# Chunk attention and HyperMixer on one Trainium2 core: 12 loads a batch, heads h and h+4 on two partition halves, block-diagonal v, three score units a batch, joint w_q/w_k projection

## The chip, the cores and the metric

One core of one Trainium2 chip. The metric is device time in microseconds of one execution. A profiled execution also gives the span from the first to the last instruction, which is about 2 us shorter. TensorE's clock is granted by a throttle; the profile shows it by slice of time.

## The reference, cut to what matters

```python
# q, k, v: (8 batches, 8 heads, 576, 64) float32
def _attn_ref(q, k, v):                       # chunks of 64, nine a head
    scores = scale * np.matmul(q_c, k_c.transpose(0, 1, 2, 4, 3))
    ...                                       # softmax over each chunk
    return np.matmul(attn, v_c)

def _moe_ref(x, w_q, w_k, w_out):             # x: (8, 576, 512)
    wq, wk = x @ w_q, x @ w_k                 # 512 -> 64 each
    W_tok = scale * np.einsum('bsd,btd->bst', wq, wk)
    mixed = np.einsum('bst,btd->bsd', W_tok, x)
    return np.maximum(mixed, 0.0) @ w_out     # 512 -> 512
```

The kernel does not form W_tok: it computes G = wk^T x first (64 x 512), then wq G. It works in float16 with float32 accumulation.

## The kernel before

The order of all work is fixed in a string, `PLAN`. A token is a unit, and the digit behind the colon is the slot of a ring of four PSUM tiles (128 x 2 x 512 float32) that it uses: `Tq00` transposes one part of q, `S` computes scores and the exponential, `A` multiplies by v and divides by the sum, `X` transposes, `Q`, `K`, `G` and `M` are the mixer up to the relu, `O` is one 128-row output block.

All inputs are loaded by GpSimd, which casts them to float16. A batch has 16 loads, each on all 128 partitions:

```python
def load_qk(b, part):                      # parts of 5 and 4 row blocks
    a, e = TR[part]
    for src, dst in ((qf, qn), (kf, kn)):
        for t in range(a, e, 2):           # rows of 1 KB
            x = min(t + 2, e)
            nc.gpsimd.dma_start(dst[b][part][:, t - a : x - a, :], ...[:, t:x, :])

def load_v(b, lo, hi):
    for t in range(lo, hi, 6):             # rows of 256 B
        nc.gpsimd.dma_start(vt[b][:, t : t + 6, 0:D], ...[:, t : t + 6, :])
```

An attend unit takes two heads. A chunk is a 64-row, 65-column matmul (64 columns of v and one of ones); rows and columns of the array are both used in halves, and a unit is 20 matmuls, two of them padding:

```python
for c in (2 * jj, 2 * jj + 1):
    half = CH * (g % 2)
    lhsT = est[...][half : half + CH, ...]
    rhs = vt[b][half : half + CH, g // 2, 0 : D + 1]
    nc.tensor.matmul(a[CH * (c % 2) : CH * (c % 2) + CH, hh, jj * W : jj * W + D + 1], lhsT=lhsT, rhs=rhs, ...)
```

Q is projected with a doubled w_q, so that both partition halves hold it; K takes another 20 matmuls a batch. The stores are issued by SyncE. They are held back until the last load has landed: a two-element transfer (`mark`) reads the last k tile first, on the same queue, so that stores never compete with loads. An output block is written over input tiles that are no longer needed.

```python
nc.scalar.copy(os_, a[:, 0, :])
if n == GATE:
    nc.sync.dma_start(mark[:], kn[B - 1][1][0:1, 0, 0:2])
nc.sync.dma_start(of[n * P : n * P + P, :], os_)
```

The softmax here doesn't subtract the row's maximum and nothing guards it: scores larger than these inputs give would overflow.

## Time and profile before

| | before |
|---|---|
| median of 3 runs | 136.05 us (134.57 to 137.67) |
| profiled span | 133.2 us |
| GpSimd issues loads until | 100.8 us |
| first output store | 104.4 us |
| TensorE ends | 127.6 us |

The page of the profile of before. First the busy time of each engine, then three of its rows over 40 slices of the span (busy tenths of TensorE, granted clock in tenths, GB/s moved), then the chain that ended last, by engine:

```profile
PE 107.0 (80%) x2479; PEld 65.6 (49%) x2479; DVE 77.7 (58%) x132; ACT 67.6 (51%) x117; POOL 97.8 (73%) x138
...
PE   6924397069999698999969987999999599999930
...
PEclk9995558965899975799999998699999999999995
...
GB/s 11 144 128 166 126 117 186 165 137 164 164 142 152 167 157 138 152 169 149 142 162 168 135 161 154 153 148 153 160 131 154 119 374 339 383 340 383 388 381 150
...
POOL 51%; PE 30%; DMA 9%; issue 3%; DVE 3%; ACT 0%; DVEq 0%; POOLq 0%
```

TensorE is busy 80% of the time, but the chain is 51% GpSimd (POOL). In the row of GB/s there are two regimes behind the start: about 120 to 190 GB/s (counted in float16, half of what is read) for four fifths of the span, then 340 to 390 GB/s of stores.

The timeline of GpSimd in before, one batch (start, duration, engine, line, operation, output and input, count; an idle time before the group would stand in brackets):

```profile
57.23 5.01 POOL L113 DMA_DIRECT2D vt<-in_v_dram  x6
62.11 1.54 POOL L106 DMA_DIRECT2D qn<-in_q_dram  x2
63.52 1.57 POOL L106 DMA_DIRECT2D kn<-in_k_dram  x2
64.94 2.16 POOL L106 DMA_DIRECT2D qn<-in_q_dram  x3
66.93 2.15 POOL L106 DMA_DIRECT2D kn<-in_k_dram  x3
68.89 5.11 POOL L113 DMA_DIRECT2D vt<-in_v_dram  x6
```

There is no idle time: the next load is issued as soon as the last one has been. From one v group to the next it is 11.66 us. The starts also give the time of one load: with 256 rows about 0.70 us, with 768 rows 0.81 us, so rows are cheap and instructions are dear.

The waits of before, on the engines and on the store queue (total us, times, longest):

```profile
DVE kT L153 <- DMA kn<-in_k_dram: 13.9, 13, 4.1
...
DVE qT L153 <- DMA qn<-in_q_dram: 11.5, 5, 4.3
```

```profile
SPq L314 <- DMA kn<-in_k_dram: 102.9, 1, 102.9
SPq L315 <- ACT rmx L288: 2.9, 5, 1.3
```

VectorE, which transposes q and k, waits 25.4 us for loads. The stores wait 102.9 us for the last k load. The first output store in the queue's timeline:

```profile
104.42 0.65 SPq L315 DMA_DIRECT2D out_dram<-qn  x1
```

### The profile page before, as it was taken

The page shows a single profiled execution, that of the slowest core. Times are in us where ns is not written, and L with a number is a line of the kernel's source. Part 1 is how long each engine was busy: PE and PEld are TensorE (multiplying, and loading weights), DVE is VectorE, ACT ScalarE, POOL GpSimd, SP SyncE. Part 2 cuts the span into 40 slices and gives each one's busy share as a digit, 9 for nine tenths or more (in the row PEclk, how much of TensorE's full clock was granted, in tenths as well). Part 3 has the DMA queues.
Part 4 walks back from the last instruction along what each step waited for, and adds up shares of the span by engine and source line. Part 5 has one row for each costly group of instructions (what it writes and reads, how often), then busy time and mean ns, then how long its engine had stood idle before and what let it go on. Part 6 is the DMA issues. An engine that isn't in the chain of part 4 may idle for free.

```text
span 133.2 us, 5640 instructions
## 1 busy us (share of the span) xinstructions
PE 107.0 (80%) x2479; PEld 65.6 (49%) x2479; DVE 77.7 (58%) x132; ACT 67.6 (51%) x117; POOL 97.8 (73%) x138
## 2 busy tenths in 40 slices
PE   6924397069999698999969987999999599999930
PEld 2303275054367346566746655557657276643400
DVE  3151685244888767697677967587895776500000
ACT  3003121037653655348637673558758367579830
POOL 6999996999999999999999999998992000000000
PEclk9995558965899975799999998699999999999995
DMA  0999999999999999999999999999999399999993
GB/s 11 144 128 166 126 117 186 165 137 164 164 142 152 167 157 138 152 169 149 142 162 168 135 161 154 153 148 153 160 131 154 119 374 339 383 340 383 388 381 150
DMA packets 64669, 24.69 MB, mean 185 GB/s; under 512 B 41092, under 2 KB 60036, under 8 KB 64644
## 3 DMA queue, kind: packets, MB, share of 16 engines
q0 software_dynamic: 59456, 14.89, 118.5%
q1 hardware_dynamic: 5188, 9.44, 19.0%
q8 instruction: 19, 0.31, 1.0%
q14 instruction: 6, 0.05, 0.1%
HBM read 29.75 MB, written 9.44 MB: 294 GB/s over the span
## 4 chain that ended last, share of the span: by engine, by line
POOL 51%; PE 30%; DMA 9%; issue 3%; DVE 3%; ACT 0%; DVEq 0%; POOLq 0%
POOL vt L113 22%; POOL qn L106 14%; PE ring L300 13%; POOL kn L106 13%; DMA wout<-in_moe_w_out_dram 5%; DMA kn<-in_k_dram 4%; PE ring L176 3%; PE ring L240 3%; PE ring L266 2%; PE ring L230 2%; PE ring L280 2%; PE ring L207 2%; DVE xt L235 2%; PE ring L252 1%; DVE kT L153 1%
## 5 line engine op out<-in xcount | busy, mean ns | idle before, releaser
L113 POOL DMA_DIRECT2D vt<-in_v_dram x48 | 40.5, 952 | 1.8 <-DMA wout<-in_moe_w_out_dram 1.2
L300 PE MATMUL ring<-wout,rmx 128*128 128x512 f16 x144 | 37.6, 400 | 0.2
L184 ACT ACTIVATE est<-ring 128x640 f16<-128x640 f32 (+1 forms) x32 | 19.3, 650 | 25.5 <-PE ring L176 24.7
L106 POOL DMA_DIRECT2D qn<-in_q_dram x40 | 29.9, 845 | 0.8 <-POOLq L348 0.8
L106 POOL DMA_DIRECT2D kn<-in_k_dram x40 | 30.0, 844 | 0.0
L153 DVE STREAM_TRANSPOSE kT<-kn 128x640 f32<-128x640 f32 (+1 forms) x16 | 19.4, 1215 | 14.0 <-DMA kn<-in_k_dram 13.9
L217 DVE TENSOR_TENSOR xn<-ring,rec 128x640 f16<-128x640 f32 x32 | 26.4, 824 | 1.2
L176 PE MATMUL ring<-qT,kT 32*64 32x64 f16 x1152 | 15.6, 215 | 13.4 <-DVE qT L153 4.9
L288 ACT ACTIVATE rmx<-ring 128x576 f16<-128x576 f32 x32 | 19.9, 653 | 5.0 <-PE ring L280 4.7
L176 PEld LDWEIGHTS <-kT 32*64 32x64 f16 x1152 | 13.6, 115 | 17.6 <-DVE kT L153 10.2
L300 PEld LDWEIGHTS <-rmx 128*128 128x128 f16 x144 | 12.9, 100 | 15.0 <-issue 3.4
L153 DVE STREAM_TRANSPOSE qT<-qn 128x640 f32<-128x640 f32 (+1 forms) x16 | 12.3, 770 | 11.8 <-DMA qn<-in_q_dram 11.5
L235 DVE COPY xt<-ring 128x1280 f16<-128x1280 f16 x16 | 12.8, 810 | 1.6 <-PE ring L230 1.5
L312 ACT COPY qn<-ring 128x512 f32<-128x512 f32 x16 | 9.4, 588 | 7.3 <-PE ring L300 5.9
L207 PE MATMUL ring<-vt,est 64*64 64x65 f16 x576 | 12.0, 211 | 1.3 <-ACT est L184 1.1
L230 PE MATMUL ring<-ident,xn 128*128 128x128 f16 x160 | 12.3, 230 | 0.4 <-DVE xn L217 0.3
L312 ACT COPY kn<-ring 128x512 f32<-128x512 f32 x16 | 9.4, 589 | 6.4 <-PE ring L300 6.2
L207 PEld LDWEIGHTS <-est 64*64 64x64 f16 x576 | 8.5, 120 | 7.3 <-issue 3.6
L247 ACT CAST wqT<-ring 128x576 f16<-128x576 f32 x8 | 5.1, 639 | 13.7 <-PE ring L240 13.7
L230 PEld LDWEIGHTS <-xn 128*128 128x128 f16 x160 | 10.3, 103 | 2.4 <-issue 0.6
L216 DVE RECIPROCAL rec<-ring 128x10 f32<-128x10 f32 x32 | 6.5, 202 | 7.6 <-PE ring L207 7.1
L240 PE MATMUL ring<-xt,wqd 128*128 128x288 f16 x64 | 9.7, 293 | 1.3 <-DVE xt L235 1.3
(30 smaller groups left out, 76.0 us busy)
## 6 DMA issues: line engine op xcount, KB each, us to landing
vt<-in_v_dram POOLq DMA_DIRECT2D x48, 96.0 KB, 4.2
qn<-in_q_dram POOLq DMA_DIRECT2D x32, 128.0 KB, 4.5
kn<-in_k_dram POOLq DMA_DIRECT2D x32, 128.0 KB, 4.6
out_dram<-qn SPq DMA_DIRECT2D x16, 256.0 KB, 3.7
out_dram<-kn SPq DMA_DIRECT2D x16, 256.0 KB, 3.7
out_dram<-spare SPq DMA_DIRECT2D x4, 256.0 KB, 3.4
qn<-in_q_dram POOLq DMA_DIRECT2D x8, 64.0 KB, 4.5
kn<-in_k_dram POOLq DMA_DIRECT2D x8, 64.0 KB, 4.3
```

The lines of the kernel that those rows point to most:

```text
L106: nc.gpsimd.dma_start(dst[b][part][:, t - a : x - a, :], src[b].rearrange("(t p r) d -> p t (r d)", p=P, r=R)[:, t:x, :],)
L113: nc.gpsimd.dma_start(vt[b][:, t : t + 6, 0:D], vf[b].rearrange("(t p) d -> p t d", p=P)[:, t : t + 6, :],)
L153: nc.vector.transpose(out=o, in_=src[b][part].bitcast(F32).rearrange("p t (r d) -> p t r d", d=32))
L176: nc.tensor.matmul(a[CH * ch : CH * ch + CH, i, (t - t0) * CH : (t - t0) * CH + CH], lhsT=k_of(b, t, 2 * rows + i, ch, e), rhs=q_of(b, t, ...
L184: nc.scalar.activation(est[b % 2][s].rearrange("p i t c -> p i (t c)")[:, :, 0:n], a[:, :, 0:n], AF.Exp, scale=scale_attn,)
L207: nc.tensor.matmul(a[CH * (c % 2) : CH * (c % 2) + CH, hh, jj * W : jj * W + D + 1], lhsT=lhsT, rhs=rhs, start=True, stop=True,)
L217: nc.vector.tensor_tensor(out=xn[b % 2][:, :, 2 * kk * D : 2 * kk * D + 2 * D].rearrange("p j (i d) -> p i j d", i=2), in0=xv[:, :, :, 0:D ...
L230: nc.tensor.transpose(tx[:, i, j * P : j * P + P], xn[b % 2][:, j, (2 * n + i) * P : (2 * n + i) * P + P], ident[:],)
L235: nc.vector.tensor_copy(xt[b % 2][n][:], tx[:, :, 0 : NJ * P])
L288: nc.scalar.activation(rmx[(b // 2) % 2].rearrange("p (h i) n -> p i h n", h=2)[:, i, :, o : o + HS], a[:, :, 0:HS], AF.Relu, scale=scale_moe,
L300: nc.tensor.matmul(a[:, 0, :], lhsT=rmx[pr % 2][:, i, tl * P : tl * P + P], rhs=wout[:, i, :], start=(i == 0), stop=(i == NI - 1),)
L312: nc.scalar.copy(os_, a[:, 0, :])
```

## The change

It is meant to put heads h and h+4 on the two partition halves. Then the 64 x 64 exponentials of two heads lie above each other, and one 128-row matmul against a block-diagonal v (v of head h top left, of head h+4 bottom right, two columns of ones) does for both. Scores come in three units of 768 columns a batch instead of four. w_q and w_k are projected together; K is then turned by matmuls with a part of the identity, and Q is evicted twice, once for each half. v has four buffers instead of eight. The loads become 12 a batch, each on 64 partitions. `PLAN` is a new order.

```diff
-        for src, dst in ((qf, qn), (kf, kn)):
-            for t in range(a, e, 2):
-                nc.gpsimd.dma_start(dst[b][part][:, t - a : x - a, :], ...)
+        for src, dst in ((q, qn), (k, kn)):
+            for u in range(2):
+                nc.gpsimd.dma_start(dst[b][part][CH * u : CH * u + CH, 0 : e - a, :], ...)
...
+    def load_v(b):
+        for n in range(0, NP, NP // 2):
+            for u in range(2):
+                nc.gpsimd.dma_start(
+                    vt[b % VB][CH * u : CH * u + CH, n : n + NP // 2, D * u : D * u + D], ...)
+    def clear_v(i, on_scalar):             # zeros and ones of the block-diagonal v
...
-    TR = ((0, 5), (5, NT))
+    TR = [((0, 3), (3, NT))] + [((0, 6), (6, NT))] * (B - 1)
...
+    def attend(b, h, a):
+        for c in range(2 * NJ):
+                lhsT = est[b % 2][t // TS][:, x // 2, 2 * (t % TS) + x % 2, :]
+                rhs = vt[b % VB][:, m, :]
+            nc.tensor.matmul(af[CH * (c % 2) : CH * (c % 2) + CH, o : o + W], lhsT=lhsT, rhs=rhs, ...)
...
-                    lhsT=wqd[:, i, :],
+                    lhsT=wqk[:, i, :],
-        nc.scalar.copy(wqT[b % 2]..., a[:, :, 0:HS])
+        nc.scalar.copy(wT[b % 2][:, 0:S]..., a[:, :, 0:HS])
+        nc.scalar.copy(wq2[b % 2][CH:, :]..., a[0:CH, :, 0:HS])
...                                        # mlp_k
-            for i in range(NI):
-                    lhsT=xt[b % 2][i // 2][:, i % 2, j * P : j * P + P],
-                    rhs=wk[:, i, :],
+                lhsT=wT[b % 2][:, j * P : j * P + P],
+                rhs=ident[:, DH:],
```

The rule of the stores stays: none before the last load has landed.

More of the change, by code (lines that the diff above doesn't have):

```diff
@@ L17 @@
 PLAN = """
-Tq00 Tk00 Tq10 S10:0 S00:1 Tk10 A00:2 S20:3 S30:0 A10:1 F:2 A20:2 A30:3 X00:0 X10:1 Tk01
-Tq01 Q0:2 K0:3 S11:0 S01:1 G0:2 A01:3 Tq11 M00:0 Tk11 A11:1 Tq02 M10:2 M20:0 Tk02 M30:3
-O:2 S31:0 S21:3 O:2 O:1 A21:0 A31:3 O:2 X01:1 S02:0 S12:2 X11:3 A02:0 K1:1 Tq12 Tk12
-Q1:2 G1:3 A12:0 Tq03 M01:1 M11:2 S22:3 Tk03 S32:1 X02:0 M21:2 O:3 S13:1 A22:2 S03:0
-A32:3 O:1 A03:2 M31:0 X12:3 Tq13 Tk13 A13:1 O:0 O:2 K2:3 Q2:0 S33:2 S23:1 Tq04 Tk04 G2:3
-O:0 A23:2 M02:1 M12:3 X03:0 A33:1 S04:2 S14:3 Tq14 O:0 X13:2 A04:1 M22:3 Tk14 O:0 Q3:2
-K3:3 M32:1 A14:0 S24:2 Tk05 S34:3 G3:1 O:0 A24:2 M03:3 Tq05 O:1 M13:0 A34:3 X04:2 S05:1
-S15:0 Tq15 X14:3 O:1 Tk15 O:2 K4:0 M23:3 A05:1 S25:2 Tq06 S35:0 G4:3 A15:1 M33:2 Q4:0
-A25:3 A35:2 X05:1 O:0 O:3 M04:2 M14:0 Tk06 O:1 X15:3 S06:2 S16:0 O:1 Tk16 Tq16 K5:3
-M24:2 A06:0 S36:1 S26:3 O:2 G5:0 M34:1 Tk07 A16:3 A26:2 Q5:0 Tq07 O:1 M05:3 A36:0 Tq17
-O:2 M15:1 Tk17 S17:3 S07:0 X16:2 X06:1 O:3 M25:2 A07:0 S27:1 K6:3 A17:2 S37:0 G6:1 M35:3
-A27:0 A37:2 Q6:1 O:3 M06:0 M16:1 X17:2 X07:3 O:0 O:2 K7:1 Q7:3 M26:0 M36:2 G7:1 O:3 O:0
-M07:2 M17:1 O:3 O:0 O:2 M27:1 M37:3 O:0 O:2 O:1 O:3 O:0
+Tq00 Tk00 F:0 Tq10 S00:0 A00:1 Tk10 S20:2 S10:3 Tq01 A30:0 Tk01 A10:1 A20:2 S11:3 S01:0
+X10:1 X00:3 A11:2 Tq11 Tk11 A01:0 Q0:1 S21:3 Tq02 K0:2 X01:0 Tk02 G0:1 A21:3 A31:2 M00:0
+M10:1 S02:0 S12:1 O:3 X11:0 M20:2 A12:1 Tk12 M30:3 Q1:0 O:2 Tq12 K1:3 A02:1 S22:0 G1:3
+Tq03 O:2 Tk03 M01:1 M11:0 X02:3 O:2 A32:1 S13:0 S03:3 A22:2 O:1 Tq13 M21:0 M31:3 Tk13
+X12:2 O:1 A13:0 A03:3 Tq04 S23:2 Q2:1 O:0 O:2 Tk04 O:3 K2:1 A23:0 S04:2 A33:3 G2:1 X03:0
+M02:2 M12:1 X13:3 Tk14 M22:0 Tq14 S14:2 A04:1 M32:3 O:0 Q3:2 S24:3 Tq05 O:1 K3:0 O:2 O:3
+Tk05 A34:0 A24:1 G3:2 S05:3 S15:0 A14:2 M03:1 X14:3 Tk15 M13:0 Tq15 X04:2 M23:1 M33:3
+O:0 S25:1 Tq06 A05:3 A15:2 Q4:0 O:1 Tk06 O:3 O:0 K4:2 A25:1 S16:3 A35:0 G4:2 S06:1 X05:3
+Tk16 M04:2 M14:0 X15:1 Tq16 M24:3 O:2 M34:0 A16:3 A06:1 S26:2 Q5:0 O:3 Tk07 O:2 Tq07
+K5:1 O:0 A36:3 A26:2 G5:1 S07:0 S17:3 Tq17 X06:1 X16:2 M05:0 M15:3 Tk17 O:1 A17:0 A07:2
+S27:3 Q6:1 A37:0 O:3 K6:2 A27:1 M25:0 M35:3 G6:2 X07:0 X17:1 M06:3 M16:2 O:0 Q7:3 O:1
+K7:2 O:0 M26:3 M36:2 G7:1 O:0 O:3 M07:2 M17:1 O:0 O:3 O:2 M27:1 M37:0 O:3 O:2 O:1 O:0
+O:3
 """
@@ L54 @@
     R = 4
-    NT = H * S // (P * R)
-    NV = H * S // P
+    NP = H * NCH // 2
+    NT = NCH
     NI = DM // P
     HS = S // 2
-    W = D + 2
+    W = 2 * D + 2
+    WS = 172
+    VB = 4
     scale_attn = 1.0 / math.sqrt(D)
     scale_moe = 1.0 / math.sqrt(DH)
-    TR = ((0, 5), (5, NT))
+    TS = 3
+    TR = [((0, 3), (3, NT))] + [((0, 6), (6, NT))] * (B - 1)
     sb = ctx.enter_context(tc.tile_pool(name="sb", bufs=1))
@@ L69, in each @@
         return [sb.tile(shape, dt, name=f"{name}{i}") for i in range(n)]
-    qn = [[sb.tile([P, e - a, R * D], F16, name=f"qn{i}_{a}") for a, e in TR] for i in range(B)]
-    kn = [[sb.tile([P, e - a, R * D], F16, name=f"kn{i}_{a}") for a, e in TR] for i in range(B)]
-    vt = each(B, [P, NV, W], F16, "vt")
-    wqd = sb.tile([P, NI, 2 * DH], F16, name="wqd")
-    wk = sb.tile([P, NI, DH], F16, name="wk")
+    qn = [
+        [sb.tile([P, max(e - a, 4), R * D], F16, name=f"qn{i}_{a}") for a, e in TR[i]]
+        for i in range(B)
+    ]
+    kn = [
+        [sb.tile([P, max(e - a, 4), R * D], F16, name=f"kn{i}_{a}") for a, e in TR[i]]
+        for i in range(B)
+    ]
+    vt = each(VB, [P, NP, W], F16, "vt")
+    wqk = sb.tile([P, NI, 2 * DH], F16, name="wqk")
     wout = sb.tile([P, NI, DM], F16, name="wout")
@@ L82 @@
     kT = each(2, [P, NT * R * D], F16, "kT")
-    est = [each(4, [P, 2, 5, CH], F16, f"est{i}_") for i in range(2)]
-    rec = each(2, [P, 2, NJ], F32, "rec")
+    est = [each(NT // TS, [P, 2, 2 * TS, CH], F16, f"est{i}_") for i in range(2)]
+    rec = each(2, [P, NJ, 2], F32, "rec")
     xn = each(2, [P, NJ, DM], F16, "xn")
     xt = [each(2, [P, 2, NJ * P], F16, f"xt{i}_") for i in range(2)]
-    wqT = each(2, [P, S], F16, "wqT")
+    wT = each(2, [P, NJ * P], F16, "wT")
+    wq2 = each(2, [P, S], F16, "wq2")
     wkn = each(2, [P, NJ, DH], F16, "wkn")
@@ L92 @@
     mark = sb.tile([1, 2], F16, name="mark")
-    GATE = 0
     ring = [ps.tile([P, 2, 512], F32, name=f"ring{i}") for i in range(4)]
-    qf = q.rearrange("b h s d -> b (h s) d")
-    kf = k.rearrange("b h s d -> b (h s) d")
-    vf = v.rearrange("b h s d -> b (h s) d")
     of = out.rearrange("b s m -> (b s) m")
     def load_qk(b, part):
-        a, e = TR[part]
-        for src, dst in ((qf, qn), (kf, kn)):
-            for t in range(a, e, 2):
-                x = min(t + 2, e)
+        a, e = TR[b][part]
@@ L106, in load_qk @@
+        for src, dst in ((q, qn), (k, kn)):
+            for u in range(2):
                 nc.gpsimd.dma_start(
-                    dst[b][part][:, t - a : x - a, :],
-                    src[b].rearrange("(t p r) d -> p t (r d)", p=P, r=R)[:, t:x, :],
-                )
-    def load_v(b, lo, hi):
-        for t in range(lo, hi, 6):
-            nc.gpsimd.dma_start(
-                vt[b][:, t : t + 6, 0:D],
-                vf[b].rearrange("(t p) d -> p t d", p=P)[:, t : t + 6, :],
-            )
+                    dst[b][part][CH * u : CH * u + CH, 0 : e - a, :],
+                    src[b]
+                    .rearrange("h s d -> (h s) d")
+                    .rearrange("(u t p r) d -> u p t (r d)", u=2, t=NT, r=R)[u][:, a:e, :],
+                )
@@ new lines, in load_v @@
+    def load_v(b):
+        for n in range(0, NP, NP // 2):
+            for u in range(2):
+                nc.gpsimd.dma_start(
+                    vt[b % VB][CH * u : CH * u + CH, n : n + NP // 2, D * u : D * u + D],
+                    v[b]
+                    .rearrange("h s d -> (h s) d")
+                    .rearrange("(u g p) d -> u p g d", u=2, p=CH)[u][:, n : n + NP // 2, :],
+                )
+    def clear_v(i, on_scalar):
+        for h in range(2):
+            o = vt[i][CH * h : CH * h + CH]
+            z = D - D * h
+            if on_scalar:
+                nc.scalar.copy(
+                    o.bitcast(F32)[:, :, z // 2 : z // 2 + D // 2],
+                    zero.bitcast(F32)[CH * h : CH * h + CH, None, 0 : D // 2].broadcast_to(
+                        [CH, NP, D // 2]
+                    ),
+                )
+            else:
+                nc.vector.memset(o[:, :, z : z + D], 0.0)
+            nc.vector.memset(o[:, :, 2 * D + h], 1.0)
+            nc.vector.memset(o[:, :, 2 * D + 1 - h], 0.0)
@@ L118, with load @@
+    def load(b):
+        load_qk(b, 0)
+        load_v(b)
+        if b == 1:
+            nc.gpsimd.dma_start(wout[:], moe_w_out.rearrange("(i p) m -> p i m", p=P))
+        load_qk(b, 1)
     nc.vector.memset(zero[:], 0.0)
-    load_qk(0, 0)
-    load_v(0, 0, NV // 2)
-    load_qk(0, 1)
-    load_v(0, NV // 2, NV)
+    for i in range(VB):
+        clear_v(i, i > 1)
+    load(0)
     make_identity(nc, ident[:])
-    wqv = moe_w_q.rearrange("(i p) j -> p i j", p=P)
-    nc.gpsimd.dma_start(wqd[:, :, 0:DH], wqv)
@@ L126 @@
-    nc.gpsimd.dma_start(wqd[:, :, DH:], wqv)
-    nc.gpsimd.dma_start(wk[:], moe_w_k.rearrange("(i p) j -> p i j", p=P))
-    nc.gpsimd.dma_start(wout[:], moe_w_out.rearrange("(i p) m -> p i m", p=P))
-    for b in range(1, B):
-        load_qk(b, 0)
-        load_v(b, 0, NV)
-        load_qk(b, 1)
-    for i in range(B):
-        nc.vector.memset(vt[i][:, :, D:], 1.0)
-    nc.vector.memset(padl[:], 1.0 / CH)
+    for w, o in ((moe_w_q, 0), (moe_w_k, DH)):
+        nc.gpsimd.dma_start(wqk[:, :, o : o + DH], w.rearrange("(i p) j -> p i j", p=P))
@@ L137 @@
+    for b in range(1, VB):
+        load(b)
+    for i in range(2):
+        nc.vector.memset(wT[i][:, S:], 0.0)
+    nc.vector.memset(padl[:], 1.0 / P)
     nc.vector.memset(padr[:], 0.0)
-    nc.vector.memset(padr[:, D:], 1.0)
+    nc.vector.memset(padr[:, 2 * D :], 1.0)
     def fill(a, n):
@@ L145, in tr @@
         part = int(which[1])
-        a, e = TR[part]
+        a, e = TR[b][part]
         src, dst = (qn, qT) if which[0] == "q" else (kn, kT)
@@ L153, in tr @@
         nc.vector.transpose(
-            out=o, in_=src[b][part].bitcast(F32).rearrange("p t (r d) -> p t r d", d=32)
+            out=o,
+            in_=src[b][part].bitcast(F32)[:, 0 : e - a, :].rearrange("p t (r d) -> p t r d", d=32),
         )
@@ L169, in scores @@
     def scores(b, s, a):
-        rows, part = s % 2, s // 2
-        t0, t1 = TR[part]
-        for t in range(t0, t1):
-            for e in range(2):
-                for ch in range(2):
-                    for i in range(2):
-                        nc.tensor.matmul(
-                            a[CH * ch : CH * ch + CH, i, (t - t0) * CH : (t - t0) * CH + CH],
-                            lhsT=k_of(b, t, 2 * rows + i, ch, e),
-                            rhs=q_of(b, t, 2 * rows + i, ch, e),
-                            start=(e == 0),
-                            stop=(e == 1),
-                        )
-        n = (t1 - t0) * CH
+        for t in range(TS):
+            for ch in range(2):
+                for e in range(2):
+                    for i in range(2):
+                        for u in range(2):
+                            o = (2 * t + ch) * CH
+                            nc.tensor.matmul(
+                                a[CH * u : CH * u + CH, i, o : o + CH],
+                                lhsT=k_of(b, TS * s + t, 2 * u + i, ch, e),
+                                rhs=q_of(b, TS * s + t, 2 * u + i, ch, e),
+                                start=(e == 0),
+                                stop=(e == 1),
+                            )
         nc.scalar.activation(
-            est[b % 2][s].rearrange("p i t c -> p i (t c)")[:, :, 0:n],
-            a[:, :, 0:n],
+            est[b % 2][s].rearrange("p i t c -> p i (t c)"),
+            a[:, :, 0 : 2 * TS * CH],
             AF.Exp,
@@ L189, in scores @@
         )
-    def attend(b, kk, a):
-        for jj in range(NJ):
-            for hh in range(2):
-                for c in (2 * jj, 2 * jj + 1):
-                    g = NCH * (2 * kk + hh) + c
-                    half = CH * (g % 2)
-                    if c < NCH:
-                        t, m = g // 8, g % 8
-                        part = 0 if t < TR[0][1] else 1
-                        lhsT = est[b % 2][2 * part + m // 4][
-                            half : half + CH, (m // 2) % 2, t - TR[part][0], :
-                        ]
-                        rhs = vt[b][half : half + CH, g // 2, 0 : D + 1]
-                    else:
-                        lhsT = padl[half : half + CH, :]
-                        rhs = padr[half : half + CH, 0 : D + 1]
-                    nc.tensor.matmul(
-                        a[CH * (c % 2) : CH * (c % 2) + CH, hh, jj * W : jj * W + D + 1],
-                        lhsT=lhsT,
-                        rhs=rhs,
-                        start=True,
-                        stop=True,
-                    )
-        xv = a[:, :, 0 : NJ * W].rearrange("p i (j c) -> p i j c", c=W)
-        rc = rec[kk % 2]
-        nc.vector.reciprocal(rc[:], xv[:, :, :, D])
-        nc.vector.tensor_tensor(
-            out=xn[b % 2][:, :, 2 * kk * D : 2 * kk * D + 2 * D].rearrange(
-                "p j (i d) -> p i j d", i=2
-            ),
-            in0=xv[:, :, :, 0:D],
-            in1=rc[:, :, :, None].broadcast_to([P, 2, NJ, D]),
@@ new lines, in attend @@
+    def attend(b, h, a):
+        af = a.rearrange("p i c -> p (i c)")
+        for c in range(2 * NJ):
+            m = NCH * h + c
+            if c < NCH:
+                t, x = m // 4, m % 4
+                lhsT = est[b % 2][t // TS][:, x // 2, 2 * (t % TS) + x % 2, :]
+                rhs = vt[b % VB][:, m, :]
+            else:
+                lhsT, rhs = padl[:], padr[:]
+            o = (c // 2) * WS
+            nc.tensor.matmul(
+                af[CH * (c % 2) : CH * (c % 2) + CH, o : o + W],
+                lhsT=lhsT,
+                rhs=rhs,
+                start=True,
+                stop=True,
+            )
+        xv = af[:, 0 : NJ * WS].rearrange("p (j c) -> p j c", c=WS)
+        rc = rec[h % 2]
+        nc.vector.reciprocal(rc[:], xv[:, :, 2 * D : W])
+        nc.vector.tensor_tensor(
+            out=xn[b % 2]
+            .rearrange("p j (u h d) -> p j u h d", u=2, d=D)[:, :, :, h, :],
+            in0=xv[:, :, 0 : 2 * D].rearrange("p j (u d) -> p j u d", u=2),
+            in1=rc[:, :, :, None].broadcast_to([P, NJ, 2, D]),
@@ L231, in xtr @@
                     tx[:, i, j * P : j * P + P],
-                    xn[b % 2][:, j, (2 * n + i) * P : (2 * n + i) * P + P],
+                    xn[b % 2][:, j, (2 * i + n) * P : (2 * i + n) * P + P],
                     ident[:],
@@ L235, in xtr, with mlp_w @@
         nc.vector.tensor_copy(xt[b % 2][n][:], tx[:, :, 0 : NJ * P])
-    def mlp_q(b, a):
+    def mlp_w(b, a):
         for i in range(NI):
@@ L241, in mlp_q @@
                     a[:, h, 0:HS],
-                    lhsT=wqd[:, i, :],
-                    rhs=xt[b % 2][i // 2][:, i % 2, h * HS : h * HS + HS],
+                    lhsT=wqk[:, i, :],
+                    rhs=xt[b % 2][i % 2][:, i // 2, h * HS : h * HS + HS],
                     start=(i == 0),
@@ L246, in mlp_q @@
                 )
-        nc.scalar.copy(wqT[b % 2].rearrange("p (h n) -> p h n", h=2), a[:, :, 0:HS])
+        nc.scalar.copy(
+            wT[b % 2][:, 0:S].rearrange("p (h n) -> p h n", h=2), a[:, :, 0:HS]
+        )
+        nc.scalar.copy(
+            wq2[b % 2][CH:, :].rearrange("p (h n) -> p h n", h=2), a[0:CH, :, 0:HS]
+        )
     def mlp_k(b, a):
         for j in range(NJ):
-            for i in range(NI):
-                nc.tensor.matmul(
-                    a[:, 0, j * DH : j * DH + DH],
-                    lhsT=xt[b % 2][i // 2][:, i % 2, j * P : j * P + P],
-                    rhs=wk[:, i, :],
-                    start=(i == 0),
-                    stop=(i == NI - 1),
-                )
+            nc.tensor.matmul(
+                a[:, 0, j * DH : j * DH + DH],
+                lhsT=wT[b % 2][:, j * P : j * P + P],
+                rhs=ident[:, DH:],
+                start=True,
+                stop=True,
+            )
         nc.vector.tensor_copy(
-            wkn[b % 2].rearrange("p j c -> p (j c)"), a[:, 0, 0 : NJ * DH]
+            wkn[b % 2][:],
+            a[:, 0, 0 : NJ * DH].rearrange("p (j c) -> p j c", c=DH),
         )
@@ L282, in mix @@
                 lhsT=g16[b % 2][CH * h : CH * h + CH, i * P : i * P + P],
-                rhs=wqT[b % 2][CH * h : CH * h + CH, half * HS : half * HS + HS],
+                rhs=(wT, wq2)[h][b % 2][CH * h : CH * h + CH, half * HS : half * HS + HS],
                 start=True,
@@ L312, in outp, with flush @@
         nc.scalar.copy(os_, a[:, 0, :])
-        if n == GATE:
+        held.append((of[n * P : n * P + P, :], os_))
+        if done.get(B - 1 - VB) == 4:
+            flush()
+    held = []
+    def flush():
+        if "gate" not in done:
+            done["gate"] = 1
             nc.sync.dma_start(mark[:], kn[B - 1][1][0:1, 0, 0:2])
-        nc.sync.dma_start(of[n * P : n * P + P, :], os_)
-    unit = {"S": scores, "A": attend, "X": xtr, "M": mix, "Q": mlp_q, "K": mlp_k, "G": mlp_g}
+        for dst, src in held:
+            nc.sync.dma_start(dst, src)
+        held.clear()
+    unit = {"S": scores, "A": attend, "X": xtr, "M": mix, "Q": mlp_w, "K": mlp_k, "G": mlp_g}
     fill(ring[0], 7)
@@ L332 @@
         else:
-            unit[u[0]](int(u[2]), int(u[1]), a)
+            b = int(u[2])
+            unit[u[0]](b, int(u[1]), a)
+            if u[0] == "A":
+                done[b] = done.get(b, 0) + 1
+                if done[b] == 4 and b + VB < B:
+                    load(b + VB)
+                    if b + VB == B - 1:
+                        flush()
 _INS = ['q', 'k', 'v', 'moe_w_q', 'moe_w_k', 'moe_w_out']
```

## The prediction

> **What bounds the kernel now.** Two transfers in series, not the matmuls. The chain of waits is 51% GpSimd, all input loads, and 30% TensorE. GpSimd's timeline shows loads back to back to 100.8 us: per batch ten q and k loads (6.85 us) and six v loads of 0.82 us, 11.76 us in all. VectorE's transposes idle 25.4 us for them (list of waits), and the first output store waits until 103.6 us for the last k load (the store queue's waits). Then 9.44 MB of stores run mostly at 365 to 390 GB/s, to about 131.5. So the span of 133.2 is about 104 of loading plus 28 of storing. TensorE ends at 127.6: the compute tail only just hides beside the stores.
>
> **What changes.**
> - Loads: 12 instructions a batch instead of 16, the same rows of 1 KB (q, k) and 256 B (v), but each on 64 partitions. Before's durations are 0.60 us at 128 rows, 0.70 at 256, 0.75 at 512, 0.82 at 768: nearly fixed cost. From them I estimate 0.62, 0.69 and 0.95 us for the new 192, 384 and 1152 rows: 9.0 us a batch on GpSimd, 2.7 less. The transfer engines cannot follow fully: packets recorded in before peak near 375 a us for q and k and 1,130 for v; 2,304 and 4,608 a batch make an estimated 10.2 us. So the bound moves to the transfer engines.
> - Risk: the Trainium skill, "DMA: Bandwidth & Descriptors", Rules for kernel authors, says transfers to disjoint partition halves serialise and advises one 128-partition transfer. No run here shows yet whether halves are slower. I allow 0.3 to 0.5 us a batch.
> - TensorE: attend has 320 matmuls of 130 columns instead of 640 of 65 (18.7 us busy). The skill, "TensorEngine Tiling (Array Packing)", Instruction Overhead, gives about 60 cycles a matmul, so 65 columns were hardly over the floor: I expect 10 to 17 us. K goes from 160 matmuls (6.3 us) to 40 (about 1.7). Scores stay 1,152, with four row groups in turn: 15.6 to perhaps 12. In all 8 to 14 of 107 us.
> - ScalarE gains a second projection eviction (8 x 0.64 us) and zero fills at the start: about +8 us busy, off the path. VectorE: about 4 us of zero fills, while it waits for loads anyway.
>
> **On the critical path.** Only the loading rate: 8 x (11.76 - 10.6) = 9 us, plus 2 to 3 for fewer instructions before batch 1 and the stall on wout there. Last landing at about 92 instead of 103.5. TensorE's savings are worth little alone, but let it follow faster loads (13.4 us busy a batch before). The tail after the last load stays about 28 us.
>
> **Prediction.** 123.5 us (136.05 before), 8 in 10 between 117 and 131. Faster by over 2%: 0.90; within 2%: 0.07; slower: 0.03.
>
> **What would show it.** GpSimd loads of 0.6 to 1.0 us with idle time between, waiting for earlier loads to land (landing over 5 us, before 4.2 to 4.6). First store at 90 to 96. Stores still at about 380 GB/s for 25 to 28 us. TensorE busy 93 to 100. VectorE's waits for q and k loads still the largest data waits.
>
> **What would make it wrong.** Half-partition loads running slower (q and k under 300 packets a us): then 130 to 137. GpSimd costing per row rather than per instruction. Compute, with four PSUM slots in a fixed order, failing to keep a batch in 10.6 us, so that stores wait for it: 126 to 131. No congestion at all: 116.

## The result, and the profile after

| | before | changed |
|---|---|---|
| median us | 136.86 (4 runs) | 124.44 (4 runs, 123.47 to 125.27) |
| ratio of the fast runs | | 0.919 (95%: 0.905 to 0.934) |
| profiled span, us | 133.2 | 122.5 |
| first output store, us | 104.4 | 91.2 |
| from first store to the end of the span, us | 28.8 | 31.3 |

Ratios here and below are the mean time of one kernel's fast runs over that of before's fast runs of the same rounds, so they are not quite the ratios of the medians.

The span fell by 10.7 us: the stores start 13.2 us earlier, and the stage behind that became 2.5 us longer. The same rows of the page of the changed kernel:

```profile
PE 101.7 (83%) x2039; PEld 64.4 (53%) x2039; DVE 82.9 (68%) x146; ACT 76.4 (62%) x121; POOL 71.2 (58%) x105
...
PE   6912246497679996999999999999999999999970
...
PEclk9995555557999999589999999999999999999998
...
GB/s 10 125 142 176 183 195 168 168 200 191 176 164 168 174 160 177 199 162 176 179 176 155 191 184 159 189 191 164 168 48 314 361 375 366 383 386 146 335 277 165
...
PE 59%; POOL 15%; DMA 14%; issue 4%; DVE 4%; ACT 2%; DVEq 0%; ACTq 0%; POOLq 0%
PE ring L325 26%; DMA wout<-in_moe_w_out_dram 8%; PE ring L203 7%; PE ring L228 7%; POOL vt L120 6%; PE ring L260 6%; DMA vt<-in_v_dram 5%; PE ring L250 5%; POOL kn L110 4%; PE ring L305 4%; POOL qn L110 3%; PE ring L291 3%; DVE xt L255 2%; POOL wqk L156 1%; PE ring L276 1%
```

The chain is now 59% TensorE and 15% GpSimd. Read in order of time it is TensorE's work from 39 us to 118.7 us, but for about 7 us in four places, the longest from 92.35 to 95.94 us (VectorE, and "issue", time with no wait that the profile shows). The row of TensorE is at 9 nearly throughout from the seventeenth slice on, and at the end the rate drops to 146 and 277 GB/s: the stores now wait for results.

The timeline of GpSimd in the changed kernel, one batch:

```profile
59.40 3.51 POOL L120 DMA_DIRECT2D vt<-in_v_dram  x4
62.87 1.26 POOL L110 DMA_DIRECT2D qn<-in_q_dram  x2
64.10 1.25 POOL L110 DMA_DIRECT2D kn<-in_k_dram  x2
65.93 0.69 POOL L110 DMA_DIRECT2D qn<-in_q_dram  x1 [0.57 <-DMA vt<-in_v_dram]
67.31 0.66 POOL L110 DMA_DIRECT2D qn<-in_q_dram  x1 [0.69 <-DMA vt<-in_v_dram]
68.40 0.66 POOL L110 DMA_DIRECT2D kn<-in_k_dram  x1 [0.43 <-DMA vt<-in_v_dram]
69.34 0.66 POOL L110 DMA_DIRECT2D kn<-in_k_dram  x1 [0.29 <-DMA vt<-in_v_dram]
69.99 3.41 POOL L120 DMA_DIRECT2D vt<-in_v_dram  x4
```

This batch takes 10.59 us; the five from 28.8 to 80.4 us take 9.5 to 10.9, 10.3 in the mean. GpSimd is busy for 8.6 us of it; the brackets are idle time in which it waits for earlier loads to land. A load of 192 rows takes 0.63 us, of 384 rows 0.66, of 1152 rows 0.87.

The waits of the changed kernel, and its first output store, as above:

```profile
DVE qT L179 <- DMA qn<-in_q_dram: 3.8, 3, 2.2
```

```profile
91.17 0.69 SPq L349 DMA_DIRECT2D out_dram<-qn  x1
```

```profile
SPq L347 <- DMA kn<-in_k_dram: 89.6, 1, 89.6
SPq L349 <- ACT qn L337: 5.1, 5, 2.0
SPq L349 <- ACT rmx L313: 2.1, 5, 0.7
SPq L349 <- ACT kn L337: 2.1, 4, 1.0
```

VectorE's largest wait for loads fell from 13.9 to 3.8 us. The stores' waits for ScalarE's evictions add up to 12.8 us (all seven lines, three shown), in before to 6.4.

### The profile page after: what moved, and what is told of

It is laid out like the page before. It is cut to its first block, busy times and chain, and to the rows that moved or that the text cites. A ratio compares the mean times of both kernels' runs of the same rounds, so it can differ in the third digit from the quotient of the medians.

```text
span 122.5 us, 4768 instructions
## 1 busy us (share of the span) xinstructions
PE 101.7 (83%) x2039; PEld 64.4 (53%) x2039; DVE 82.9 (68%) x146; ACT 76.4 (62%) x121; POOL 71.2 (58%) x105
## 4 chain that ended last, share of the span: by engine, by line
PE 59%; POOL 15%; DMA 14%; issue 4%; DVE 4%; ACT 2%; DVEq 0%; ACTq 0%; POOLq 0%
PE ring L325 26%; DMA wout<-in_moe_w_out_dram 8%; PE ring L203 7%; PE ring L228 7%; POOL vt L120 6%; PE ring L260 6%; DMA vt<-in_v_dram 5%; PE ring L250 5%; POOL kn L110 4%; PE ring L305 4%; POOL qn L110 3%; PE ring L291 3%; DVE xt L255 2%; POOL wqk L156 1%; PE ring L276 1%
## 5 line engine op out<-in xcount | busy, mean ns | idle before, releaser
L210 ACT ACTIVATE est<-ring 128x768 f16<-128x768 f32 x24 | 18.9, 810 | 22.1 <-PE ring L203 21.7
L203 PE MATMUL ring<-qT,kT 32*64 32x64 f16 x1152 | 16.9, 214 | 13.4 <-DVE kT L179 7.6
L120 POOL DMA_DIRECT2D vt<-in_v_dram x32 | 27.3, 876 | 0.8 <-PE ring L325 0.5
L110 POOL DMA_DIRECT2D qn<-in_q_dram x32 | 21.2, 677 | 8.4 <-DMA vt<-in_v_dram 7.6
L110 POOL DMA_DIRECT2D kn<-in_k_dram x32 | 20.7, 654 | 5.5 <-DMA vt<-in_v_dram 3.4
L325 PEld LDWEIGHTS <-rmx 128*128 128x128 f16 x144 | 13.1, 99 | 14.3 <-issue 2.0
L179 DVE STREAM_TRANSPOSE kT<-kn 128x384 f32<-128x384 f32 (+1 forms) x16 | 19.5, 1221 | 0.6 <-DMA kn<-in_k_dram 0.4
L228 PE MATMUL ring<-vt,est 128*64 128x130 f16 x288 | 14.8, 240 | 1.2 <-ACT est L210 1.2
L179 DVE STREAM_TRANSPOSE qT<-qn 128x384 f32<-128x384 f32 (+1 forms) x16 | 12.2, 764 | 3.8 <-DMA qn<-in_q_dram 3.8
L228 PEld LDWEIGHTS <-est 128*64 128x64 f16 x288 | 11.1, 119 | 4.9 <-issue 1.9
L260 PE MATMUL ring<-xt,wqk 128*128 128x288 f16 x64 | 9.6, 295 | 0.1
L267 ACT CAST wT<-ring 128x576 f16<-128x576 f32 x8 | 5.1, 639 | 7.2 <-PE ring L260 7.2
```

Of the source, the lines that this page charges most:

```text
L110: nc.gpsimd.dma_start(dst[b][part][CH * u : CH * u + CH, 0 : e - a, :], src[b] .rearrange("h s d -> (h s) d") .rearrange("(u t p r) d -> u ...
L120: nc.gpsimd.dma_start(vt[b % VB][CH * u : CH * u + CH, n : n + NP // 2, D * u : D * u + D], v[b] .rearrange("h s d -> (h s) d") .rearrange ...
L179: nc.vector.transpose(out=o, in_=src[b][part].bitcast(F32)[:, 0 : e - a, :].rearrange("p t (r d) -> p t r d", d=32),)
L203: nc.tensor.matmul(a[CH * u : CH * u + CH, i, o : o + CH], lhsT=k_of(b, TS * s + t, 2 * u + i, ch, e), rhs=q_of(b, TS * s + t, 2 * u + i, ...
L210: nc.scalar.activation(est[b % 2][s].rearrange("p i t c -> p i (t c)"), a[:, :, 0 : 2 * TS * CH], AF.Exp, scale=scale_attn,)
L228: nc.tensor.matmul(af[CH * (c % 2) : CH * (c % 2) + CH, o : o + W], lhsT=lhsT, rhs=rhs, start=True, stop=True,)
```

## The experiments

Every kernel was timed beside the kernel before on the same chip. The runs were made on three chips: the control, e6, e7 and e9 on one, e1 to e4 on another, e5, e8, b1 and b2 on a third; so across these groups the ratios are to be trusted before the medians. "Control" is the changed kernel run again. In the profiled execution of four (e7, e8, b1, b2) and of e2 the time was over 1.5% above the fastest run of that kernel; where their traces are used, that is said. Differences between two kernels are given by the ratios, that is by fast runs (a difference of 0.01 is 1.36 us), and by the medians where that is said.

| run | what it is | median us | ratio to before (95%) |
|---|---|---|---|
| a0_after | control | 125.66 | 0.926 (0.921 to 0.931) |
| e1_full12 | before, 12 loads a batch, 128 partitions | 131.83 | 0.962 (0.947 to 0.977) |
| e2_half12 | before, 12 loads a batch, 64 partitions | 132.80 | none computed |
| e3_after_small | changed, 22 small loads a batch | 139.19 | 1.029 (1.017 to 1.041) |
| e4_before_half_loaded | before, batches 4 to 7 not loaded | 126.95 | 0.938 (0.929 to 0.948) |
| e5_after_half_loaded | changed, batches 4 to 7 not loaded | 127.63 | 0.944 (0.939 to 0.949) |
| e6_after_64row | changed, v not block-diagonal | 132.98 | 0.970 (0.964 to 0.975) |
| e7_after_sep_k | changed, K projected apart | 126.67 | 0.930 (0.924 to 0.935) |
| e8_64row_half_loaded | e6, batches 4 to 7 not loaded | 129.49 | 0.956 (0.950 to 0.963) |
| e9_after_fills_late | changed, zero fills moved | 127.19 | 0.938 (0.934 to 0.941) |
| b1_no_pads | changed, no padding matmuls | 129.51 | 0.948 (0.941 to 0.956) |
| b2_no_pads_late_wout | b1, w_out loaded later | 132.78 | 0.966 (0.959 to 0.974) |

### The control

> The changed kernel itself, as the control for the runs beside it. 124.4 us, ratio to the kernel before about 0.92. All theories expect the same.

Measured: 125.66 us. The ratio of 0.926 lies inside the interval of the first result (0.905 to 0.934). First store at 93.3 us in its trace.

### Loads alone: e1_full12 and e2_half12

My theory: the number of load instructions bounded the first 104 us. The rival: the transfers themselves did, and the gain is in compute. A second rival, for the half partitions: they are slower of themselves.

```diff
 # e1: two pieces a part for q and k, four for v, on 128 partitions
-            for t in range(a, e, 2):
-                x = min(t + 2, e)
+            for t, x in ((a, (a + e + 1) // 2), ((a + e + 1) // 2, e)):
...
-        for t in range(lo, hi, 6):
+        for t in range(lo, hi, 9):
 # e2: the same number of loads, each on 64 partitions with twice the row blocks
+            for o in (slice(0, CH), slice(CH, P)):
...
-        for t in range(lo, hi, 6):
+        for t in range(lo, hi, 18):
+            for o in (slice(0, CH), slice(CH, P)):
```

> The kernel before, with only its loads changed: 12 a batch on 128 partitions instead of 16 (q and k in two pieces a part, v in four of 1152 rows), everything else as it was. Theory (issue of loads is what bounds the first 104 us of before): GpSimd about 9.1 us a batch, first store at 90 to 93 us instead of 103.6, but then TensorE with its old work ends last: 126 to 130 us. Rival (loads are bound by the transfers themselves, and the gain of the change is in compute): first store over 100 us, within 2 us of the kernel before.

> As e1_full12, the same number and size of loads, but each on 64 partitions with twice the rows for each. Theory: half-partition loads cost nothing of their own: first store within 1.5 us of e1_full12 and the time within 1 us of it. Rival (disjoint halves serialise and are slower): first store 4 us or more later than in e1_full12, packets of q and k under 300 a us.

Measured: 131.83 us and 132.80 us. The store queue's timeline, first e1, then e2:

```profile
91.33 0.72 SPq L313 DMA_DIRECT2D mark<-kn  x1
92.18 0.65 SPq L314 DMA_DIRECT2D out_dram<-qn  x1
```

```profile
90.64 0.72 SPq L314 DMA_DIRECT2D mark<-kn  x1
91.49 0.65 SPq L315 DMA_DIRECT2D out_dram<-qn  x1
```

(e2's execution is one of those 1.5% over its fastest; three of its four runs, this one included, lie between 132.75 and 132.86 us.) Both start to store at 91.5 to 92.2 us, as the changed kernel does. So with the same bytes the loading rate follows the number of load instructions, and half-partition loads show no cost here: e2 is even 0.7 us earlier, and its q and k packets reach 381 in one us, not under 300. That part of the theory holds, by one trace of each; the times can't say more, as e2 has one fast run (130.59 us) against e1's two (129.42 and 130.52). But e1's time fell by only 5 us by the ratio (3 to 7 by its interval), 4 by the medians, not by the 11 to 12 us that I had counted for the loads; its median lies above the 126 to 130 us that I expected, its fast runs at the upper end. The stage from the first store to the end is 35.5 us in e1's trace instead of 28.8: with the old compute the work is not done when the stores could go.

### The changed kernel with slow loads: e3_after_small

```diff
-            for u in range(2):
+            for u, x in [(u, x) for x in range(a, e, 3) for u in range(2)]:
...
-        for n in range(0, NP, NP // 2):
+        for n in range(0, NP, NP // 3):
```

> The changed kernel with its loads cut smaller, 22 a batch instead of 12, with the same bytes, so that by before's durations GpSimd needs about 12.4 us a batch, as much as before. Theory: first store at 102 to 106 us, stores as fast as ever, 133 to 137 us: the whole gain goes. Rival (the gain is in compute): 124 to 128.

Measured: 139.19 us, 29.3 us from the first store to the end of the span:

```profile
108.30 0.67 SPq L349 DMA_DIRECT2D out_dram<-qn  x1
```

GpSimd was busy 98.0 us. Time and first store are both later than I expected (133 to 137 and 102 to 106), and later than before's: between v groups it is 11.9 to 13.1 us from 35 to 85 us of the timeline, in before 11.7 to 12.4 from 45 to 93. The whole gain goes with the loading rate. The faster loads are therefore needed for the gain, but by e1 they are not enough for it.

### Compute without loads: e4_before_half_loaded and e5_after_half_loaded

```diff
-    for b in range(1, B):
+    for b in range(1, 4):                  # e4; in e5 load(b + VB) goes
         load_qk(b, 0)
...
-            in_=src[b][part]...
+            in_=src[b % 4][part]...
+    hq, hk = ...                           # output blocks have tiles of their own
```

> The kernel before with wrong results on purpose: batches 4 to 7 are computed from the data of batches 0 to 3, so loading ends at about 50 us, and the rest shows how fast compute alone is. Theory: from 44 to 104 us TensorE of before idles only about 6.5 us, so the time falls to 125 to 129 us only, which is what faster loads alone could give. Rival (compute has large slack under the loads): under 120.

> The changed kernel with wrong results on purpose: batches 4 to 7 computed from the data of batches 0 to 3, so loading ends at about 48 us. Theory: the changed kernel's chain is TensorE work without a break from 39 us, so with half the loads gone the time hardly falls: 122.5 to 125. Rival (the loads still set the time of the changed kernel): under 120.

Measured: e4 126.95 us, as expected. Faster loads alone could not have brought before under about 127 us. Still, e1 stays 3 us above that by the ratios, 5 by the medians, with all its loads landed by 92 us; this distance is taken up below.

e5 missed: 127.63 us, 2.4 us over the control by the ratios, 2.0 by the medians. My edit is partly to blame. Batch 4 took the tiles of batch 0, which are cut three and six instead of six and three row blocks, so a long transpose came just before its scores. The trace has one stop of TensorE for it:

```profile
64.67 0.85 PE L205 MATMUL ring<-qT,kT 32*64 32x64 f16 x48 [2.92 <-DVE qT L181]
```

This stop is not in the control. It makes e5 a poor floor. Less the stop, an estimate would be 127.6 - 2.9 = 124.7 us, near the control and far from the rival's 120: loads after about 50 us hardly set the time of the changed kernel.

### Attend undone: e6_after_64row

The changed kernel's chain has ten block-diagonal matmuls in 0.41 us, where 20 small ones took 0.28 to 0.32 in before's. So I expected attend to have become a loss on TensorE, and its undoing to win 3 us.

```diff
-                lhsT = est[b % 2][t // TS][:, x // 2, 2 * (t % TS) + x % 2, :]
-                rhs = vt[b % VB][:, m, :]
+                    u = (c + f) % 2
+                    o = slice(CH * u, CH * u + CH)
+                        lhsT = est[b % 2][t // TS][o, x // 2, 2 * (t % TS) + x % 2, :]
+                        rhs = vt[b % VB][o, m, 0 : D + 1]
...                                        # v buffers 66 columns wide, no zero fills
```

> The changed kernel with v no longer block-diagonal: attend goes back to 64-row, 65-column matmuls, 20 a unit on the four quadrants, and the zero fills go. Theory: in the changed kernel's chain ten block-diagonal matmuls take 0.41 us, where 20 small ones took 0.28 to 0.32 before, so block-diagonal v cost TensorE about 0.1 us a unit, 3.2 us in all, and TensorE is what ends last now: about 121 us, with attend units back at about 0.3 us. Rival (the 128-row contraction is part of the gain, as the change intends and as my prediction allowed): slower than the changed kernel by 1 us or more.

Measured: 132.98 us. My theory fell: undone, attend makes the kernel 5.9 us slower (0.0435 x 135.9), 7.3 by the medians. And yet its units did take 0.28 us, and TensorE was not busy for longer. First the control, then e6:

```profile
PE 100.5 (81%) x2039; PEld 63.9 (52%) x2039; DVE 82.4 (67%) x146; ACT 76.4 (62%) x121; POOL 71.3 (58%) x105
```

```profile
PE 99.8 (77%) x2359; PEld 61.2 (47%) x2359; DVE 77.1 (60%) x130; ACT 71.7 (56%) x117; POOL 71.2 (55%) x105
```

Stretches of TensorE's timeline in e6 (idle time before a group in brackets, and what ended it):

```profile
23.68 0.38 PE L213 MATMUL ring<-vt,est 64*64 64x65 f16 x13 [3.69 <-issue]
...
29.87 0.38 PE L235 MATMUL ring<-ident,xn 128*128 128x128 f16 x4 [2.51 <-issue]
...
40.04 0.30 PE L186 MATMUL ring<-qT,kT 32*64 32x64 f16 x9 [1.05 <-issue]
...
56.44 0.48 PE L186 MATMUL ring<-qT,kT 32*64 32x64 f16 x26 [1.32 <-issue]
```

```profile
78.76 0.42 PE L290 MATMUL ring<-wT,g 64*128 64x288 f16 x1 [2.57 <-issue]
78.76 0.42 PE L290 MATMUL ring<-wq,g 64*128 64x288 f16 x1
...
90.31 0.31 PE L186 MATMUL ring<-qT,kT 32*64 32x64 f16 x11 [1.60 <-issue]
```

"issue" means that the engine waited for nothing that the profile shows. These stops break up a group of matmuls (11 of 48 scores come after the last). I counted matmuls and weight loads in the trace up to each stop, and looked for the transfers of the queue that the page calls "instruction":

```
e6: stop ends after   447   703  1214  1982  3006  3518 TensorE instructions
    idle before, us   3.7   2.5   1.1   1.3   2.6   1.6
    ends later than the start of a 16,384-byte packet of the instruction queue by
                      2.8   2.5   2.3   2.8   2.4   2.5 us
```

The counts differ by 256, 511, 768, 1024 and 512. The Trainium skill, "Runtime: NRT & Kernel Launch", Instruction fetch mechanics, says that an engine's instructions are refilled in 16 KiB blocks of 256 while the current block runs, and that a boundary costs a step that is "mostly hidden". The traces agree with the block: before has 19 packets on that queue for 4,958 matmuls and weight loads (19.4 times 256), the changed kernel 16 for 4,078 (15.9 times). They do not agree with "hidden" here.

An estimate from the durations in the chains: a unit of 48 scores is 96 instructions in 0.62 us. With a changed attend unit (20 instructions, 0.41 us) behind each, 256 instructions last 2.3 us; with e6's (40 instructions, 0.28 us), 1.7 us. From the start of a fetch to the end of a stop it takes 2.3 to 2.8. So in a dense stretch attend by halves runs out of instructions sooner than block-diagonal attend, although it needs less time on the array.

Where e6 loses its time can be read from the traces, as both kernels run the same `PLAN`: I set the ends of their 1,152 score matmuls against each other. e6 is 0.7 us ahead of the control at score 192 (control at 25.6 us), 2.8 behind at score 384 (37.5 us), after its stops of 2.5 and 1.1 us, 1.7 behind at score 816 (72.2 us), 5.5 at score 864, after the stop of 2.6 us, and 5.6 at the last (99.4 us), as in the span. Of the 3.8 us more between scores 816 and 864 the stop itself is 2.6; from 78.7 to 82.1 us e6 has half clock, which the control has nowhere after 29.5 us.

### Does the stop need the loads: e8_64row_half_loaded

The page counts the packets of the instruction queue on the same 16 transfer engines as those of the loads. New theory: the loads delay the fetch. Rival: the small matmuls cost this in any case. The edit is e6 with that of e5.

> e6_after_64row (640 more TensorE instructions than the changed kernel, 7.3 us slower) with the same half of the loads gone, wrong on purpose. New theory: e6 loses its time in stops of TensorE for its own instructions: its trace stops at instruction counts that lie multiples of 256 apart, each time until 2.3 to 2.9 us after the start of a 16 KB transfer on the instruction queue, while input loads fill the same engines. So without loads the stops after 50 us go, and the distance to e5_after_half_loaded falls from 7.3 us to under 4. Rival (the instruction count or the small matmuls cost this whatever the loads do): the distance stays at 6 us or more, with stops after 60 us as in e6.

Measured: 129.49 us; the distance to e5 is 1.6 us (0.0119 x 135.6), 1.9 by the medians, instead of 5.9 and 7.3. e8's profiled execution is a slow one (131.2 us), but it has no such stop after its loads end (50.4 us; before that it has stops of 3.8, 2.5 and 3.0 us): its one long stop behind 60 us comes after 2,332 instructions, off the series, and is the one that my cut of batch 4 makes in e5 as well. Set against e5 score by score, e8 is 7.0 us behind at score 432 (43.9 us), while loads run, and after that it falls back no more: at the last it is 3.4 behind. This agrees with e4 and e1, which run the same TensorE program: e1, with loads, has stops of 1.2, 0.9, 2.0, 0.5 and 0.9 us after 1,726, 2,493, 2,749, 3,005 and 3,261 instructions; e4, whose loads land by 58.5 us, has one of 0.5 us at 1,726 and none of 0.35 us or more behind it. That is 5.4 us against 0.5, and the times differ by 3.2 us by the ratios and 4.9 by the medians. TensorE's waits for "issue" in e1; before's list has none:

```profile
PE ring L175 <- issue: 3.3, 3, 2.0
...
PE ring L206 <- issue: 2.0, 2, 1.2
...
PE ring L279 <- issue: 0.3, 1, 0.3
```

The traces also show what it is that the loads lengthen. It is not the fetch packet: that takes 0.95 us (median) in e6 while loads run, and 0.96 in e8 after they have landed. It is the time until the fetch starts. From the crossing of one boundary to the start of the next packet it is 3.0 us in e6 (median, 40 to 91 us) and 1.0 in e8 after its loads; 2.6 in e1 and 0.9 in e4 after its loads; and 1.7 in before, whose loads come more slowly. From that start to the next boundary it is never less than 2.2 us in any of these stretches. (Boundaries are counted in recorded instructions, of which a few are missing.) So a block of 256 instructions must last some 5 us beside fast loads not to stop TensorE, by an estimate from these numbers (2.6 to 3.0 and 2.2), and 3 without. e4, e5 and e8 are not free of transfers in that stage: their stores begin at 58.8, 51.4 and 50.7 us, and TensorE does not stop for them.

### The joint projection undone: e7_after_sep_k

```diff
-                lhsT=wT[b % 2][:, j * P : j * P + P],
-                rhs=ident[:, DH:],
+            for i in range(NI):
+                    lhsT=xt[b % 2][i % 2][:, i // 2, j * P : j * P + P],
+                    rhs=wk[:, i, :],
...                                        # doubled w_q, one eviction of Q
```

> The changed kernel with w_q and w_k projected apart again (20 matmuls for K a batch, 64-column w_k, duplicate w_q, one eviction of Q on ScalarE instead of two). Theory: TensorE sets the end since about 39 us, K costs 0.58 us a batch instead of 0.14, so 8 x 0.45 = 3.5 us: 127 to 128.5. Rival (loads alone give the gain, TensorE has slack; ScalarE loses 5 us of work): 123.5 to 125.

Measured: 126.67 us, ratio 0.930 against the control's 0.926; the intervals overlap. TensorE was busy 105.2 us (in a slow execution) instead of 100.5, and nearly all of that found room, part of it perhaps because ScalarE's second eviction went. My theory fell: of its 3.5 us over the control 0.5 came by the ratios, 1.0 by the medians, which is near to the rival's slack. What the joint projection is worth is not clear of noise.

### The zero fills: e9_after_fills_late

```diff
-    for i in range(VB):
-        clear_v(i, i > 1)
+    clear_v(0, False)
...                                        # behind the token Tq10:
+                for i in range(1, VB):
+                    clear_v(i, i > 1)
```

> The changed kernel with the zero fills of v buffers 1 to 3 moved behind the first three transposes. The first transpose starts at 9.6 us in the changed kernel and 6.3 before. Theory: the first 37 us follow the loads, so the earlier start is lost again: within 0.7 us of the changed kernel. Rival (the fills delay everything behind them): up to 3 us faster.

Measured: 127.19 us, 1.6 us slower than the control. Neither expectation held. The fills were not free to move: behind the third transpose they stand between it and the next ones, and TensorE starves in slices four to seven of e9's page (the second line here), where the control's (the first) is working. Its longest stop, until k is transposed, is 12.3 us; in the control 4.2. Where the change has them, the fills lie for the most part in a time in which VectorE has no data.

```profile
PE   6912246189579997969999998999999999999970
```

```profile
PE   6940000939878999988999999799999999999970
```

### Two attempts to beat it: b1_no_pads and b2_no_pads_late_wout

```diff
-        for c in range(2 * NJ):
+        for c in range(NCH):               # b1: the last block on 64 partitions
...
-        if b == 1:                         # b2: w_out with batch 2
+        if b == 2:
```

> An attempt to beat the changed kernel: the 32 padding matmuls of attend go (the last block works on 64 partitions instead), so 64 TensorE instructions fewer and about 32 x 41 ns = 1.3 us less work on what ends last: 124 to 125 us, ratio 0.915 to 0.922. Rival (TensorE's stops hide it): no difference.

> As b1_no_pads, and the w_out load (1 MB read, GpSimd held up behind it until 28 us) moves from batch 1 to batch 2, with the first output unit moved later in the plan. Theory: the first two batches reach TensorE about 2.5 us earlier, where it starves: 122 to 124 us. Rival: the first outputs then wait for w_out, and nothing is won: 124 to 126.

Measured: 129.51 and 132.78 us; both are correct and slower than the control, by 3.0 and 5.5 us. b1 has 64 TensorE instructions fewer than the control, and less to do. Its trace, of a slow execution, has this stop, after 2,484 instructions and 2.4 us after the start of an instruction packet. Behind it a group of ten transposes takes 1.48 us, which takes 0.73 at full clock in e6's timeline:

```profile
74.31 0.30 PE L202 MATMUL ring<-qT,kT 32*64 32x64 f16 x8 [2.29 <-issue]
...
75.58 1.48 PE L246 MATMUL ring<-ident,xn 128*128 128x128 f16 x10
```

The table by stage of b1 shows the clock of that stage (busy us of PE, PEld, DVE, ACT, POOL, then the clock, 0.72):

```profile
72.00:84.00 12.00, 9.71 (x131) 5.46 (x128) 6.33 (x12) 5.66 (x9) 9.55 (x15) 0.72 1.85 174
```

Set against the control score by score, b1 is 0.1 us behind at score 768 (71.5 us), 5.2 at score 864 and 4.9 at the last: in this slow execution its whole loss lies at this stop and in the half clock behind it, from 74.4 to 81.2 us. b2's trace, a slow one too, stops for 2.0 us after 2,485 instructions and has half clock from 77.0 to 83.9 us. (Not every stop is followed by half clock: e6's of 2.6 us is, e1's of 2.0 is not.) So 64 instructions fewer can cost time, if they move a block's end into a dense stretch. I take the cause from one trace of each kernel; no run moves only the boundary, and the fast runs, which lose 3.0 and 5.5 us, were not traced, so for b1 and b2 it is argued and not shown.

## Why the prediction was right, and where it was not

The time was right (124.44 us against 123.5), and so was what was said of the pace of the loads. What was said of TensorE and of the tail was wrong, and that the sum still came out is in part luck.

- *GpSimd bounds the first 104 us by the number of its loads.* Right. e1 changes that number alone, with the same bytes, and the first store moves from 104.4 to 92.2 us; e3 raises it in the changed kernel and the first store moves to 108.3.
- *12 loads cost 9.0 us a batch, the transfers allow 10.2, with an allowance 10.6.* Right: 8.6 us busy and 9.5 to 10.9 us from batch to batch (10.3 in the mean), with idle time for landings that was not there before, and landings of 5.4 to 6.4 us instead of 4.2 to 4.6.
- *Half partitions may be slower.* They were not: e2 stores 0.7 us earlier than e1, in one trace of each.
- *First store at 90 to 96.* 91.2.
- *TensorE saves 8 to 14 us.* Wrong: 5.3 us (107.0 to 101.7; 6.5 by the control's trace). K fell, though less than expected (6.3 to 2.5 instead of 1.7). But attend rose from 12.1 to 14.9 us, and scores from 15.6 to 16.9. The prediction's 18.7 us for attend was a double count: it adds 12.0 for the matmuls and 6.7 for the padding, but these overlap in time, and all 640 together occupy 12.1. I had taken the overhead per matmul for a floor; in before's chain 20 attend matmuls on the four quadrants take 0.28 us, one every 14 ns, while the 128-row ones come every 41 ns.
- *The tail after the last load stays about 28 us, bound by the stores.* It became 31.3, and TensorE ends last. VectorE's waits for loads, which I expected to stay the largest, went from 25.4 to 4.2 us. This is the term of the sum that was mis-sized, by about 3 us.
- *On the critical path lies only the loading rate; TensorE's savings are worth little alone.* Wrong, though the sum came out, and though the prediction did say that they let TensorE follow faster loads. Of the control's 10 us, loads alone are worth 5 (e1), where I had counted 11 to 12; the other half comes only with the new compute. And that gain is not in TensorE's busy time, where I looked: the joint projection is worth half a microsecond, within noise (e7); block-diagonal v takes more busy time (15.1 us in the control, 10.2 without it in e6) and yet is worth 6 us. e6 has all of the change but that and the zero fills, and stands at 0.970, no better than e1 with its 0.962 (the intervals overlap): beside the loads, it is attend that makes the gain. What it saves is instructions in the dense stretches, and with them stops of TensorE that appear only once loads are fast and TensorE no longer waits for data. In before's list of waits no matmul waits for "issue"; in e1's, with the same TensorE program and faster loads, they do for 5.6 us in all. With half the loads gone, the old and the new compute are close (e4 126.95 us, e5 127.63, or 124.7 less its stop).

What stays open: the stops account for most of e6's loss of 5.9 us, not exactly for all. After 36 us of the span, e6 has stops of this series (of 0.35 us or more) of 6.5 us in all and the control of 1.9; the half clock after one of them costs e6 more, and a shorter attend and no zero fills stand on the other side. The new order of units was not tested alone, as it cannot be separated from the three score units; e6 against e1 shows only that order, joint projection and score units together bring no gain that can be seen beside the loads.

## What to carry to other kernels

When a bound is lifted, look at what the next one needs besides busy time. If loads bound a kernel, count their instructions, not only their bytes. And when TensorE runs many small matmuls beside heavy loading, its own instruction stream can become the limit: look for idle time ended by "issue" in the middle of a group, and for counts that repeat every 256, and prefer fewer, longer matmuls in the dense stretches even where they cost more on the array.

## What the Trainium skill lacked or had wrong

- "Runtime: NRT & Kernel Launch", Instruction fetch mechanics, has the 16 KiB block of 256 instructions, which the traces agree with, but calls the cost of a boundary "mostly hidden". With input loads running, TensorE stopped there for up to 3.7 us (e6); a stop ended 2.3 to 2.8 us after the start of the block's transfer. No page says that loads delay it: the fetch started 3.0 us after the boundary before it with loads (e6), 1.0 without (e8), and 2.6 against 0.9 in e1 and e4.
- "DMA: Bandwidth & Descriptors", Rules for kernel authors, advises one 128-partition transfer over two on disjoint halves. In this stream of queued loads halves were no slower: first store at 91.5 us with halves, 92.2 without, and GpSimd issued 1152 rows on 64 partitions in 0.88 us, on 128 partitions in 1.02.
- No page gives GpSimd's time for one load by its size. Measured here: 0.60 us for 128 rows, 0.63 for 192, 0.70 for 256, 0.66 for 384 (on 64 partitions), 0.81 for 768, 0.87 for 1152 (on 64).
- "TensorEngine Tiling (Array Packing)", Instruction Overhead, gives about 60 cycles of overhead for a matmul. It does not say there what a sequence of matmuls on different parts of the array costs, and reading it as a floor for each was my mistake, which no run here turns into one of the page: 65-column matmuls spread over the four quadrants came every 14 ns, 130-column ones on two column halves every 41 ns.
